# Moving vector-engine reductions, buffer clears and value-block steps to other places in the order of an attention and expert kernel

## Chip, cores and metric

The kernel runs on one core of a Trainium2 chip. The metric is the device time of one execution in microseconds (us).

## What is computed

Block-sparse attention for 2 batches, 8 heads, 768 positions and 64 channels, and behind it a layer of 8 experts with a top-1 router and a capacity. The reference, cut to what matters:

```python
k_sum = k.reshape(B, H, nb, block, D).max(axis=3)       # block = 32, nb = 24
v_sum = v.reshape(B, H, nb, block, D).mean(axis=3)
mask_l = np.abs(pos[:, None] - pos[None, :]) < window    # window = 16
scores_all = softmax over [masked local scores, scale * q @ k_sum.T + log(block)]
x = (a @ concat(v, v_sum)) as (1536, 512)

expert_idx = np.argmax(x @ w_gate, axis=1)               # gate_w: softmax at expert_idx
# each expert takes its first `capacity` (384) tokens in order
h = np.maximum(np.einsum('ecd,edf->ecf', disp, w1), 0.0)
y = np.einsum('ecf,efd->ecd', h, w2)
out[i] = gate_w[i] * y[expert_idx[i], pos[i]]            # 0 for tokens beyond the capacity
```

## The kernel before

**Chunks and groups.** The attention is worked off in 8 chunks c (a batch and a pair of heads). For each, SyncE loads keys `kc` (operation k), queries `qc` (q), values `v` (v) and the turned values `vc` (t). Each chunk has three groups n = 3c, 3c+1, 3c+2 of four query tiles. A group has five steps: S (L286, L287: scores and mask on TensorE), M (L291: negated row maximum on VectorE), E (L295: exponentials on ScalarE), R (L300: transposes on TensorE) and K (L304: copy to SBUF on ScalarE). V (L314) is the product with the values for one half of a chunk (V00 and V01 are the halves of chunk 0, V40 and V41 those of chunk 4), N (L322, L325) normalises it on VectorE into X.

**Inputs of a chunk.** w and kp (L229 on GpSimd) copy key windows and key-block maxima into the tile `k`; kb (L256) is the key-block maximum on VectorE. Q..v, Q..p and Q..a scale one head's queries into the tile `qb`, on VectorE, GpSimd or ScalarE. A `qb` is block-diagonal, and z2 and z3 (L222, L223) clear buffers 2 and 3 of it on GpSimd, two instructions each; buffers 0 and 1 are cleared ahead of the loop. vb (L263) sums the value blocks on VectorE, vt (L266) turns the sums on TensorE into `bank`, vk (L269) copies them to `vrow` on ScalarE, vP and vp (L229, out v<-vrow) copy them behind the values on GpSimd.

**Routes and rounds.** The first batch's 768 tokens are routed as soon as their attention is done: x, X, l, L, g (logits), ch (choice, VectorE), pf (counts and prefix sums on TensorE, into `bank`), pick (the two fullest experts of the first half, ending with the clip of the counts, `pcl`, L448), pl (places: the row maps `rowm` L425 and the column maps `colm` L428 on VectorE), tk0 (L457: product of both maps on TensorE, into `bank`), rows (`apk` L487, `aids` L494: row numbers of the expert's tokens), pads (L774 to L503), ts0 (L837) and fr0 to fr2 (L573: gathers by GpSimd's DMA queue). An expert round then works on these 384 rows while the second batch is routed: h and s split the weights, T, H, I turn and split the rows, u, r, e are the first layer (L627), D the second (L644), P scatters the result. There are three rounds. zr clears a tile of zeros that fill0 and fill1 write to the output.

**What sets the order.** Every engine works off its own queue in order. The order comes from one table, `SEQ`, whose names are called one after the other; a generator such as `pick`, `rows`, `pads`, `pl0` issues one instruction per call. Waits between engines are added by the framework from the tiles that an instruction reads and writes. `bank` is one PSUM tile with corners for logits, counts, prefix sums, the turned value sums and the token tables, and accesses of different engines to it are ordered as accesses to one tile:

```python
    bank = psum.tile([P, 4 * P], F32, name="bank", bufs=1)
    vtrn = corner(P)[:, 0]
    tbs = [corner(E, J), corner(E, J)]
```

Of the kernel before, what the change touches and what calls it, by code (L numbers as in the profile page):

```python
# [109 lines left out]


SEQ = """
q1 k1 t0 S0 k2 z2 t2 S1 M0 E0 Q11v q2 M1 Q10p w1p q3 kb1 E1 S2 kp1p vb0 R0 z3 R1 M2 t1 E2 K0 S3 K1 k3 kb2 v0 w2p vt0 M3 v2 vk0 vb2 S4 kp2p E3 v1 R2
Q21a M4 S5 q4 Q20p K2 t3 E4 Q30p vP0 k4 R3 M5 Q31a vp0 S6 vb1 E5 misc t4 R4 M6 w3p q6 S7 K3 kb3 v3 E6 vt1 M7 V00 kp3p q5 vk1 K4 V01 vp1 N00 N00 vP1 R5
N01 N01 E7 S8 K5 R6 M8 S9 K6 E8 R7 M9 vt2 vk2 V10 E9 vP2 V11 N10 N10 Q41a Q40p S10 N11 N11 K7 vp2 k5 vb3 R8 S11 M10 t5 K8 w4p kb4 E10 R9 M11 vt3 kp4p
V20 vk3 K9 vP3 V21 N20 E11 vb4 S12 vp3 N21 t6 N20 Q60p k6 Q61a N21 R10 M12 k7 R11 K10 S13 E12 vt4 K11 M13 V30 vk4 V31 E13 Q50p N30 N30 S14 N31 Q51a
N31 w5p kb5 R12 x0 M14 K12 kp5p x1 vb5 X0a x2 X1a S15 t7 vb6 X2a q7 E14 v6 vt5 M15 l00 w6p vk5 kb6 v5 R13 L00a E15 R14 w7p v4 kb7 x3 g00 K13 v7 S16
X3a kp6p vb7 K14 vP4 x4 M16 x5 Q70p X4a S17 X5a vp4 Q71a vt6 kp7p E16 M17 l01 vp5 R15 vP5 L01a E17 S18 vk6 g01 K15 M18 vp6 R16 ch0 S19 vP6 E18 ch0 ch0
ch0 ch0 R17 ch0 ch0 M19 S20 ch0 ga0 E19 ga0 ga0 pf0 ga0 pick pick pick M20 pick pick pick first lw0 lw1 lw2 lw3 vt7 V40 vk7 pl0 K16 pl0 vP7 V41 N40
pl0 K17 N40 S21 N41 vp7 zr N41 pl0 pl0 pl0 R18 pl0 pl0 E20 R19 V50 pl0 pl0 pl0 pl0 K18 M21 V51 K19 N50 N50 E21 pick tk0 S22 N51 N51 ts0 pads rows pads  # L120
R20 rows pads M22 rows fr0 S23 K20 pads E22 pads pads pads firstB R21 fr1 M23 K21 V60 E23 V61 fr2 N60 N60 h10a R22 N61 N61 R23 K22 s10v V70 K23 h11a
V71 lW0 lW1 lW2 lW3 fill0 N70 N70 x6 x7 X6a x8 X7a N71 N71 s11v x9 X8a h12p T0 x10 H0 X9a l10 X10a h13p x11 L10a T1 I0 X11a T2 H1 g10 H2 I1 l11 I2
L11a u0 s12v g11 s13v lwB0 lwB1 lwB2 lwB3 o0 o1 o2 h20a u1 ch1 ch1 r0 ch1 e0 ch1 ch1 ch1 ch1 ch1 pf1 ga1 ga1 ga1 ga1 u2 r1 e1 pl1 pl1 pl1 pl1 h21a u3
pl1 pl1 pl1 pl1 r2 e2 pl1 pl1 pl1 pl1 cl1 s20v h22a u4 r3 e3 tk1 ts1 rowsB rowsB frB0 frB1 frB2 u5 h23a r4 e4 s21v s22v u6 r5 e5 s23v padsB padsB
# [847 lines left out]
```

## Time and profile before

| | |
|---|---|
| median of 3 runs | 191.23 us (191.14 to 191.71) |
| the profiled execution | 192.58 us, span 190.5 us |
| TensorE matmul | 173.9 us busy, 91% of the span |
| VectorE | 105.3 us, 55% |
| ScalarE | 102.2 us, 54% |
| GpSimd | 61.7 us, 32% |
| DMA | 38.77 MB, mean 204 GB/s |

The span runs from the first to the last instruction; the profiled execution's own time is 2.08 us more. In the timeline a row is one instruction or several alike in a run, with the idle time of its engine ahead of it and what ended that. PE is TensorE, PEld its weight loads, DVE VectorE, ACT ScalarE, POOL GpSimd, SP SyncE.

### The profile page before, as it was taken

The numbers are of one execution on the slowest core, as the hardware profiler recorded it, in microseconds if no ns is written. First come the engines' busy times: TensorE is split into PE (matmuls) and PEld (weight loads), VectorE is DVE, ScalarE is ACT, GpSimd is POOL, SyncE is SP. The second block draws the span as 40 slices with busy tenths as digits, with TensorE's granted clock in tenths as the row PEclk, the third lists the DMA queues.
The fourth block names the chain that finished last, engine by engine and source line by source line (L and its number), as shares of the span: only waits on it lengthen the run. The fifth ranks groups of instructions, "written<-read, shape, count | busy, mean of one in ns | idle before, by whom it ended". The sixth has DMA issues, their size and how long they took to land. (4 is left out here: it accounts for less than half of the span.)

```text
span 190.5 us, 3991 instructions
## 1 busy us (share of the span) xinstructions
PE 173.9 (91%) x1461; PEld 155.7 (82%) x1461; DVE 105.3 (55%) x226; ACT 102.2 (54%) x225; POOL 61.7 (32%) x82
## 2 busy tenths in 40 slices
PE   6767999999999699899999999999999999999950
PEld 2556899999789697799998889999888899988830
DVE  3585658697279867579798658554610933210000
ACT  4549989999966496746343476444523722211110
POOL 7599528856634183000240522400022020002220
PEclk9999999999999999999999999999999999999995
DMA  5999999938949799999165899990010110001011
GB/s 169 333 322 269 256 336 288 347 139 272 276 124 322 222 341 402 401 386 368 59 163 162 315 387 383 375 369 4 0 55 0 57 59 0 0 2 57 25 40 57
DMA packets 20375, 38.77 MB, mean 204 GB/s; under 512 B 1482, under 2 KB 8572, under 8 KB 20348
## 3 DMA queue, kind: packets, MB, share of 16 engines
q1 hardware_dynamic: 18416, 33.43, 53.2%
q0 software_dynamic: 1440, 4.73, 6.8%
q10 hardware_dynamic: 492, 0.28, 0.6%
q8 instruction: 13, 0.21, 0.4%
q14 instruction: 14, 0.11, 0.2%
HBM read 29.77 MB, written 8.66 MB: 202 GB/s over the span
## 5 line engine op out<-in xcount | busy, mean ns | idle before, releaser
L644 PE MATMUL yp<-w,h 128*128 128x512 f32 x216 | 50.5, 391 | 0.0
L644 PEld LDWEIGHTS yp<-w,h 128*128 128x128 f32 x216 | 40.3, 188 | 8.2
L627 PE MATMUL hp<-xh,w1h 128*128 128x384 f32 x96 | 32.7, 340 | 0.0
L627 PE MATMUL hp<-xh,w1l 128*128 128x384 f32 x96 | 32.2, 335 | 0.0
L627 PE MATMUL hp<-xl,w1h 128*128 128x384 f32 x96 | 32.1, 335 | 0.0
L295 ACT ACTIVATE prob<-sc,nm 128x120 f32<-128x120 f32 x96 | 26.9, 369 | 8.5 <-DVE nm L291 4.6
L286 PE MATMUL sc<-k,qb 128*128 128x120 f32 x192 | 26.5, 281 | 4.4 <-ACT prob L295 1.4
L657 POOL DMA_INDIRECT out<-y,oid x9 | 9.8, 1094 | 60.5 <-ACT y L654 57.5
L286 PEld LDWEIGHTS sc<-k,qb 128*128 128x128 f32 x192 | 23.3, 191 | 6.7 <-ACT prob L295 2.0
L632 ACT ACTIVATE h<-hp 128x384 fp32r<-128x384 f32 x24 | 11.8, 492 | 29.6 <-PE hp L627 29.6
L636 DVE SCALAR_TENSOR_TENSOR h<-hp,h 128x384 fp32r<-128x384 f32 x24 | 13.3, 553 | 18.1 <-ACT h L632 18.1
L291 DVE TENSOR_REDUCE nm<-sc 128x4 f32<-128x480 f32 x24 | 15.7, 655 | 13.2 <-PE sc L287 7.6
L654 ACT ACTIVATE y<-yp,xgb 128x512 f32<-128x512 f32 x9 | 6.2, 687 | 28.4 <-PE yp L644 18.9
L627 PEld LDWEIGHTS hp<-xh,w1h 128*128 128x128 f32 x96 | 18.0, 188 | 0.3 <-issue 0.2
L627 PEld LDWEIGHTS hp<-xl,w1h 128*128 128x128 f32 x96 | 18.0, 188 | 0.1
L588 DVE TENSOR_TENSOR w<-w2r,w 128x1024 fp32r<-128x1024 f32 x12 | 14.6, 1227 | 6.1 <-ACT w L233 5.4
L627 PEld LDWEIGHTS hp<-xh,w1l 128*128 128x128 f32 x96 | 18.0, 188 | 0.0
L229 POOL TENSOR_SCALAR v<-vrow 25x1040 f32<-25x1040 f32 (+1 forms) x16 | 13.4, 840 | 10.0 <-ACT vrow L269 9.2
L582 DVE TENSOR_TENSOR w1l<-w1r,w1h 128x1024 fp32r<-128x1024 f32 x12 | 15.1, 1272 | 2.9 <-ACT w1h L233 2.7
L304 ACT COPY pts<-pt 121x512 f32<-121x512 f32 x24 | 13.9, 605 | 3.4 <-PE pt L300 2.6
L300 PE MATMUL pt<-cft,prob 128*121 128x128 f32 x96 | 14.3, 279 | 0.0
L233 ACT CAST w<-w2r 128x1024 fp32r<-128x1024 f32 x12 | 12.6, 1051 | 3.1 <-PE yp L644 2.4
(123 smaller groups left out, 223.1 us busy)
## 6 DMA issues: line engine op xcount, KB each, us to landing
w1r<-w SPq DMA_DIRECT2D x12, 512.0 KB, 7.0
w2r<-w SPq DMA_DIRECT2D x12, 512.0 KB, 6.0
v<-vw SPq DMA_DIRECT2D x16, 292.5 KB, 8.2
kc<-kT SPq DMA_DIRECT2D x8, 400.0 KB, 5.6
xrow<-x SPq DMA_DIRECT2D x2, 1542.0 KB
vc<-vT SPq DMA_DIRECT2D x8, 384.0 KB, 6.2
out<-zrow SPq DMA_DIRECT2D x2, 1536.0 KB, 12.9
qc<-qT SPq DMA_DIRECT2D x7, 384.0 KB, 6.4
```

The costliest lines, as they stand in the source:

```text
L229: eng.tensor_scalar(out=dst, in0=src, scalar1=f, scalar2=0.0, op0=ALU.mult, op1=ALU.add)
L233: nc.scalar.copy(out, in_)
L286: nc.tensor.matmul(self.sc[:, i, :], qb[c % NQ][:, t, :], kt[c][:, t, :], start=i == 0, stop=False)
L291: nc.vector.tensor_reduce(out=self.nm, in_=self.sc, op=ALU.max, axis=AX.X, negate=True)
L295: nc.scalar.activation(self.pr[:, i, :KW], self.sc[:, i], AF.Exp, bias=self.nm[:, i : i + 1])
L300: nc.tensor.transpose(self.pt[:KV, P * i : P * i + P], self.pr[:, i], ident)
L304: nc.scalar.copy(self.pts[:KV], self.pt[:KV])
L582: eng.tensor_tensor(out=self.w1l[g], in0=self.w1r[g], in1=self.w1h[g].bitcast(F32), op=ALU.subtract)
L588: eng.tensor_tensor(out=self.w2[g][:, 1], in0=self.w2r[g], in1=self.w2[g][:, 0].bitcast(F32), op=ALU.subtract)
L627: nc.tensor.matmul(ps, a[g][:, kk, fo : fo + P], x[:, kk, :], start=n == 0, stop=n == 3 * KD - 1)
L636: nc.vector.scalar_tensor_tensor(out=h[:, f % 2, 1], in0=self.hp[f], scalar=0.0, in1=h[:, f % 2, 0].bitcast(F32), op0=ALU.max, op1=ALU.sub ...
L644: nc.tensor.matmul(ps, self.h[g][:, i, a, P * j : P * j + P], self.w2[g][:, w, i, :], start=n == 0, stop=n == 3 * KF - 1)
```

## The change

Only the table `SEQ` changes; it has the same 641 names before and after. Five things move:

- z2, which stood behind the load k2, and z3, which stood behind R0, go behind E2.
- vb0 goes behind M2 (it stood ahead of R0), E2 ahead of K0, S3 ahead of K0, kb2 behind M3, S4 ahead of vb2.
- The seventh call of pick, the clip of the counts, goes from ahead of tk0 to ahead of the place steps pl0.
- vt7, vk7, vP7, vp7 and zr go from around V40 to behind R19.
- Two calls of rows go from between the calls of pads to right behind tk0.

Two places of the table:

```diff
-E1 S2 kp1p vb0 R0 z3 R1 M2 t1 E2 K0 S3 K1 k3 kb2 v0 w2p vt0 M3 v2 vk0 vb2 S4 ...
+E1 S2 kp1p R0 R1 M2 vb0 E2 z2 z3 t1 S3 K0 K1 k3 v0 w2p vt0 M3 kb2 v2 vk0 S4 vb2 ...
...
-first lw0 lw1 lw2 lw3 vt7 V40 vk7 pl0 K16 pl0 vP7 V41 N40 pl0 K17 N40 S21 N41 vp7 zr N41 ...
+pick first lw0 lw1 lw2 lw3 V40 pl0 K16 pl0 V41 N40 pl0 K17 N40 S21 N41 N41 ...
...
-R18 pl0 pl0 E20 R19 V50 ... E21 pick tk0 S22 N51 N51 ts0 pads rows pads R20 rows pads ...
+R18 pl0 pl0 E20 R19 vt7 vk7 vP7 vp7 zr V50 ... E21 tk0 rows rows S22 N51 N51 ts0 pads pads R20 pads ...
```

GpSimd at the front, before (`qb_95` are chunk 1's queries, `k_183` its keys, `qb_96` and `qb_97` are the buffers that z2 and z3 clear):

```order
L229 TENSOR_SCALAR qb_94<-qc_114 64x4x64 x3
L222 MEMSET qb_96 64x12x64
L223 MEMSET qb_96 64x12x64
L229 TENSOR_SCALAR qb_95<-qc_147 64x12x64
L229 TENSOR_SCALAR k_183<-kc_149 128x12x64
L229 TENSOR_SCALAR k_183<-kc_149 128x12x32
L229 TENSOR_SCALAR k_183<-ks 128x12x24
L222 MEMSET qb_97 64x12x64
L223 MEMSET qb_97 64x12x64
L229 TENSOR_SCALAR k_239<-kc_159 128x12x64
```

and with the change (`k_181` is chunk 1's keys here):

```order
L229 TENSOR_SCALAR qb_94<-qc_114 64x4x64 x3
L229 TENSOR_SCALAR qb_95<-qc_147 64x12x64
L229 TENSOR_SCALAR k_181<-kc_149 128x12x64
L229 TENSOR_SCALAR k_181<-kc_149 128x12x32
L229 TENSOR_SCALAR k_181<-ks 128x12x24
L222 MEMSET qb_96 64x12x64
L223 MEMSET qb_96 64x12x64
L222 MEMSET qb_97 64x12x64
L223 MEMSET qb_97 64x12x64
L229 TENSOR_SCALAR k_237<-kc_159 128x12x64
```

Chunk 1's four copies now stand ahead of all four clears, and chunk 2's keys follow the clears.

VectorE at the front, before (the rows are M1, kb1, vb0, M2, kb2, M3, vb2):

```order
L291 TENSOR_REDUCE nm<-sc 128x4
L256 TENSOR_REDUCE ks<-kc_149 128x24
L263 TENSOR_REDUCE vsq_85<-vc_151 128x24
L291 TENSOR_REDUCE nm<-sc 128x4
L256 TENSOR_REDUCE ks<-kc_159 128x24
L291 TENSOR_REDUCE nm<-sc 128x4
L263 TENSOR_REDUCE vsq_85<-vc_163 128x24
```

and with the change:

```order
L291 TENSOR_REDUCE nm<-sc 128x4
L256 TENSOR_REDUCE ks<-kc_149 128x24
L291 TENSOR_REDUCE nm<-sc 128x4
L263 TENSOR_REDUCE vsq_85<-vc_151 128x24
L291 TENSOR_REDUCE nm<-sc 128x4
L256 TENSOR_REDUCE ks<-kc_159 128x24
L263 TENSOR_REDUCE vsq_85<-vc_161 128x24
```

M2 and M3 each changed places with the reduction ahead of them.

TensorE around the first route's counts (the rows of `pf0` end above; `vsq_86` holds the sums that vt7 turns, `v_751` and `v_729` are the values of chunks 4 and 5), the piece of the difference:

```order
 L401 MATMUL bank<-oh,crt 128x8
-L266 MATMUL bank<-cft,vsq_86 128x128
 L314 MATMUL av<-v_751,pts 64x65 x24
 L286 MATMUL sc<-k_748,qb_97 128x120 x4
...
 L300 MATMUL pt<-cft,prob_83 121x128 x4
 L300 MATMUL pt<-cft,prob_84 121x128 x4
+L266 MATMUL bank<-cft,vsq_86 128x128
 L314 MATMUL av<-v_729,pts 64x65 x24
 L457 LDWEIGHTS rowm
```

vt7 goes from behind the counts to behind R19, and so vk7 on ScalarE goes from ahead of K16 to behind E20. On GpSimd nothing changes its place there: vP7, vp7 and zr stay the rows ahead of the gathers. SyncE's queue has the same rows in the same order.

VectorE from the column maps on, before:

```order
L428 TENSOR_TENSOR colm<-kt_967,eqj 128x6x24 x2
L291 TENSOR_REDUCE nm<-sc 128x4
L322 RECIPROCAL rz<-av 128x6
L325 TENSOR_TENSOR x_99<-av,rz 128x3x128
L448 TENSOR_SCALAR pcl<-bank 128x8
L322 RECIPROCAL rz<-av 128x6
L325 TENSOR_TENSOR x_99<-av,rz 128x3x128
L774 TENSOR_TENSOR mine_1089<-pcl,eq_919 128x8
L487 TENSOR_TENSOR apk<-bank,eq_919 128x24
L776 TENSOR_REDUCE c_1090<-mine_1089 128x1
L494 TENSOR_REDUCE aids<-apk 128x3
L501 TENSOR_TENSOR apad<-cft,c_1090 128x3
```

and with the change, to M22:

```order
L428 TENSOR_TENSOR colm<-kt_967,eqj 128x6x24 x2
L291 TENSOR_REDUCE nm<-sc 128x4
L322 RECIPROCAL rz<-av 128x6
L325 TENSOR_TENSOR x_99<-av,rz 128x3x128
L487 TENSOR_TENSOR apk<-bank,eq_919 128x24
L494 TENSOR_REDUCE aids<-apk 128x3
L322 RECIPROCAL rz<-av 128x6
L325 TENSOR_TENSOR x_99<-av,rz 128x3x128
L774 TENSOR_TENSOR mine_1093<-pcl,eq_919 128x8
L776 TENSOR_REDUCE c_1094<-mine_1093 128x1
L501 TENSOR_TENSOR apad<-cft,c_1094 128x3
L291 TENSOR_REDUCE nm<-sc 128x4
```

The clip `pcl` is gone from here (it stands ahead of the place steps now), and the row numbers `apk` and `aids` stand ahead of the last normalisation.

## Rows read from the trace of the kernel before

**Rows 1.** Windows: stretch, length, busy of PE, PEld, DVE, ACT, POOL, clock, DMA, GB/s.
```profile
...
24.00:56.00 32.00, 31.41 (x406) 29.13 (x403) 21.92 (x44) 27.80 (x78) 19.42 (x27) 1.00 0.87 264
...
73.00:180.00 107.00, 106.34 (x628) 96.89 (x628) 55.13 (x112) 45.61 (x70) 14.99 (x15) 1.00 0.48 172
...
```

**Rows 2.** PE timeline, front: start, length, engine, line, operation, out<-in, shapes, count, [idle<-releaser].
```profile
...
9.75 0.33 PE L287 MATMUL sc<-cmt 128*128 128x384 bf16 x1
...
12.27 1.15 PE L286 MATMUL sc<-k,qb 128*128 128x120 f32 x8 [1.04 <-POOL k L229]
...
22.55 1.62 PE L314 MATMUL av<-v,pts 121*64 121x65 f32 x48
...
```

**Rows 3.** Timeline of POOL (GpSimd), front.
```profile
...
7.82 0.73 POOL L222 MEMSET qb<- 64x768 f32 x1
8.59 1.05 POOL L223 MEMSET qb<- 64x768 f32 x1
9.73 0.82 POOL L229 TENSOR_SCALAR qb<-qc 64x768 f32<-64x768 f32 x1
10.52 1.30 POOL L229 TENSOR_SCALAR k<-kc 128x768 f32<-128x768 f32 x2
11.79 0.42 POOL L229 TENSOR_SCALAR k<-ks 128x288 f32<-128x288 f32 x1
...
```

**Rows 4.** Timeline of DVE (VectorE), front.
```profile
...
8.02 0.95 DVE L229 TENSOR_SCALAR qb<-qc 64x768 f32<-64x768 f32 x1 [0.47 <-DMA qc<-qT]
...
11.39 0.95 DVE L263 TENSOR_REDUCE vsq<-vc 128x24 f32<-128x768 f32 x1 [0.75 <-DMA vc<-vT]
12.26 0.65 DVE L291 TENSOR_REDUCE nm<-sc 128x4 f32<-128x480 f32 x1
...
```

**Rows 5.** Timeline of ACT (ScalarE), front.
```profile
...
13.03 1.11 ACT L295 ACTIVATE prob<-sc,nm 128x120 f32<-128x120 f32 x4 [2.23 <-DVE nm L291]
...
```

**Rows 6.** Timeline of SP's queue: the load of the second half of v0.
```profile
...
13.70 0.42 SPq L219 DMA_DIRECT2D v<-vw  x1
```

**Rows 7.** DMA view of that load: tile, queue, operation, count, KB, us to landing.
```profile
...
v<-vw SPq DMA_DIRECT2D x1, 292.5 KB, 8.1
```

**Rows 8.** Timeline of PE, second place.
```profile
...
56.92 0.33 PE L266 MATMUL bank<-cft,vsq 128*128 128x128 f32 x1 [0.26 <-DVE key L737]
...
64.20 0.45 PE L457 MATMUL bank<-colm,rowm 128*128 128x24 bf16 x12 [1.74 <-DVE pcl L448]
...
```

**Rows 9.** Timeline of DVE, second place.
```profile
...
57.76 1.00 DVE L747 TENSOR_TENSOR at<-eq,cft 128x16 f32<-128x16 f32 x1
...
59.00 0.45 DVE L753 TENSOR_SCALAR ei<-k 128x2 int32<-128x2 f32 x1
...
61.42 0.95 DVE L425 TENSOR_TENSOR rowm<-crt,lo 128x768 bf16<-128x768 bf16 x1
62.29 0.52 DVE L428 TENSOR_TENSOR colm<-kt,eqj 128x144 bf16<-128x144 bf16 x2
...
65.21 0.15 DVE L501 TENSOR_TENSOR apad<-cft,c 128x3 f32<-128x3 f32 x1
65.83 0.66 DVE L291 TENSOR_REDUCE nm<-sc 128x4 f32<-128x480 f32 x1 [0.47 <-PE sc L287]
...
```

**Rows 10.** Timeline of POOL, second place.
```profile
...
57.68 1.74 POOL L229 TENSOR_SCALAR v<-vrow 25x1040 f32<-25x1040 f32 x2 [3.29 <-ACT vrow L269]
...
```

**Rows 11.** Timeline of ACT, second place.
```profile
...
60.19 1.11 ACT L295 ACTIVATE prob<-sc,nm 128x120 f32<-128x120 f32 x4 [1.20 <-PE pt L300]
...
66.80 1.12 ACT L295 ACTIVATE prob<-sc,nm 128x120 f32<-128x120 f32 x4
...
73.32 1.56 ACT L233 COPY xt<-xp 128x512 f32<-128x512 f32 x3 [1.06 <-PE xp L348]
```

**Rows 12.** Timeline of all engines at the second route.
```profile
...
92.97 2.41 DVE L588 TENSOR_TENSOR w<-w2r,w 128x1024 fp32r<-128x1024 f32 x2
...
94.12 1.05 POOL L573 DMA_INDIRECT xgb<-xrow,bids  x1 [21.02 <-DMA xrow<-x]
...
```

More of the change, by code (lines that the diff above doesn't have):

```diff
@@ L112 @@
 SEQ = """
-q1 k1 t0 S0 k2 z2 t2 S1 M0 E0 Q11v q2 M1 Q10p w1p q3 kb1 E1 S2 kp1p vb0 R0 z3 R1 M2 t1 E2 K0 S3 K1 k3 kb2 v0 w2p vt0 M3 v2 vk0 vb2 S4 kp2p E3 v1 R2
+q1 k1 t0 S0 k2 t2 S1 M0 E0 Q11v q2 M1 Q10p w1p q3 kb1 E1 S2 kp1p R0 R1 M2 vb0 E2 z2 z3 t1 S3 K0 K1 k3 v0 w2p vt0 M3 kb2 v2 vk0 S4 vb2 kp2p E3 v1 R2
 Q21a M4 S5 q4 Q20p K2 t3 E4 Q30p vP0 k4 R3 M5 Q31a vp0 S6 vb1 E5 misc t4 R4 M6 w3p q6 S7 K3 kb3 v3 E6 vt1 M7 V00 kp3p q5 vk1 K4 V01 vp1 N00 N00 vP1 R5
@@ L118 @@
 X3a kp6p vb7 K14 vP4 x4 M16 x5 Q70p X4a S17 X5a vp4 Q71a vt6 kp7p E16 M17 l01 vp5 R15 vP5 L01a E17 S18 vk6 g01 K15 M18 vp6 R16 ch0 S19 vP6 E18 ch0 ch0
-ch0 ch0 R17 ch0 ch0 M19 S20 ch0 ga0 E19 ga0 ga0 pf0 ga0 pick pick pick M20 pick pick pick first lw0 lw1 lw2 lw3 vt7 V40 vk7 pl0 K16 pl0 vP7 V41 N40
-pl0 K17 N40 S21 N41 vp7 zr N41 pl0 pl0 pl0 R18 pl0 pl0 E20 R19 V50 pl0 pl0 pl0 pl0 K18 M21 V51 K19 N50 N50 E21 pick tk0 S22 N51 N51 ts0 pads rows pads
-R20 rows pads M22 rows fr0 S23 K20 pads E22 pads pads pads firstB R21 fr1 M23 K21 V60 E23 V61 fr2 N60 N60 h10a R22 N61 N61 R23 K22 s10v V70 K23 h11a
+ch0 ch0 R17 ch0 ch0 M19 S20 ch0 ga0 E19 ga0 ga0 pf0 ga0 pick pick pick M20 pick pick pick pick first lw0 lw1 lw2 lw3 V40 pl0 K16 pl0 V41 N40 pl0 K17
+N40 S21 N41 N41 pl0 pl0 pl0 R18 pl0 pl0 E20 R19 vt7 vk7 vP7 vp7 zr V50 pl0 pl0 pl0 pl0 K18 M21 V51 K19 N50 N50 E21 tk0 rows rows S22 N51 N51 ts0 pads
+pads R20 pads M22 rows fr0 S23 K20 pads E22 pads pads pads firstB R21 fr1 M23 K21 V60 E23 V61 fr2 N60 N60 h10a R22 N61 N61 R23 K22 s10v V70 K23 h11a
 V71 lW0 lW1 lW2 lW3 fill0 N70 N70 x6 x7 X6a x8 X7a N71 N71 s11v x9 X8a h12p T0 x10 H0 X9a l10 X10a h13p x11 L10a T1 I0 X11a T2 H1 g10 H2 I1 l11 I2
```

## Prediction

> **What bounds the kernel now.** I read the busy time of the engines by stage first. From 24 to 56 us TensorE is busy for 31.41 of 32.00 us and from 73 to 180 us for 106.34 of 107.00, at granted clock 1.00 [rows 1]. In both stretches TensorE sets the pace, so whatever brings it there earlier stays saved, as long as its inputs come. All of the change lies ahead of them or between them: at 7 to 24 us and at 56 to 73 us. So I read those two places engine by engine in the timeline, to see which wait ends last.
>
> At the front, TensorE waits 1.04 us at 12.27 for the keys of chunk 1 from GpSimd [rows 2]. GpSimd was late because the two clears of z2 (0.73 us each) lay ahead of its three copies for chunk 1 [rows 3]. The exponentials E2 on ScalarE wait 2.23 us for the maximum M2 on VectorE [rows 5], and VectorE was late because it took the value sums vb0 first and waited 0.75 us there for a load, though the scores S2 had been ready since 9.75 + 0.33 = 10.08 us [rows 2, 4].
>
> At the second place TensorE waits 1.74 us at 64.20 for the clip of the counts, L448 [rows 8]. The clip has nothing to do with the product that waits: both use the tile `bank`, and the row maps and column maps which the product reads were done at 62.29 + 0.52 = 62.81 us [rows 9].
>
> **Front part: z2, z3, M2, M3, S4 (forecast 1.45 us gained).**
> Step 1, chunk 1 on GpSimd. Chunk 1's queries land at 8.0 us: VectorE's half starts on them at 8.02 [rows 4]. Without z2 ahead, GpSimd's half starts there too instead of at 9.73. The two halves get in each other's way: VectorE's half took 0.95 us beside the clears, and the second clear took 1.05 us beside it, against 0.73 for the first [rows 3, 4]. I take VectorE first, for 0.55 us (between 0.42, which is what was left of it after the first clear ended, and 0.95), then 0.82 on GpSimd: 9.4 us. The copies of 1.30 us follow to 10.7. VectorE meanwhile does M1 (0.65, as M2) and the key maxima kb1 (0.95, as vb0) by 10.1, so the last copy, 0.42 us, ends at 11.1, and the scores S3 start at 11.2 instead of 12.27: 1.1 us. If GpSimd goes first, VectorE is 0.8 us later and S3 starts at about 11.65.
> Step 2, M2 ahead of vb0. M2 can start at 10.15 and ends at 10.8 us. E2 then starts at 10.9 instead of 13.03: 2.1 us. vb0 still starts at 11.39, when its load is there [rows 4], so the load train behind it in SyncE's queue (t1, k3, v0) starts as before.
> Step 3, what is late next. From E2 on, ScalarE's exponentials and copies run in one queue, and that chain moves by up to 2.1 us. But the second half of the values v0 was issued at 13.70 and took 8.1 us, so it lands at 21.8 [rows 6, 7]. The products V01 that need it are the second half of a 1.62 us group that began at 22.55 [rows 2], so they began at about 23.36. They can begin at 21.85: 1.5 us, and 1.45 after a little friction at later loads. Moving z2 and z3 together behind chunk 1 costs GpSimd 4 x 0.73 = 2.92 us from 11.1 to 14.2. Chunk 2's copies then start some 0.4 us later than before, which the queries for S6 bear: they would be ready at 16.8, and S6 waits for E4 until 17.0. Bounds: 0.5 us if later loads eat most of it, 2.1 if v0 lands earlier too, since the load q3, freed by GpSimd's first copy, goes out 1.2 us sooner.
>
> **Second part: the clip, vt7, vk7 and the copies (forecast 0.15 us lost).**
> Taken alone, the clip's move gives 1.74 us, less what the column maps leave. And vt7 leaves its place, where TensorE waited 0.26 us and worked 0.33 [rows 8], so V40 starts at 56.6, and the exponentials E20, which started at 60.19 after a transpose [rows 11], at 59.6 us. VectorE gains too. At 57.76 its product with two SBUF inputs took 1.00 us, and the cast at 59.00 took 0.45, while GpSimd's value copies ran from 57.68 for 1.74 us [rows 9, 10]; a small product of the same kind alone, at 65.21, took 0.15 [rows 9]. With the copies gone from there, everything up to the row maps moves some 0.95 us ahead (0.8 and 0.3, less 0.15 for the clip): the row maps, which began at 61.42, run from 60.47 to 61.42.
> But the copies come back at a worse place. vt7 now runs after R19, E20 ends at 60.7, vk7 takes 0.26 us, and GpSimd starts on vP7 0.08 us later: 61.1 us, in the middle of the row maps. These and the column maps have two SBUF inputs as well. GpSimd waits for the row maps to end (61.4) and makes its first, larger copy in about 1.06 us (that of before held the product of 57.76 until 58.76). One column map of 0.26 us gets through, then the second copy takes the other 0.65, then the second column map follows: done at 63.5 instead of 62.81. A row at the second route shows such a change of hands: GpSimd's gather at 94.12 started between two of VectorE's products (2.41 us for two, from 92.97) and needed 1.05 us [rows 12].
> The Trainium skill, "SBUF — State Buffer", section "Who interferes with whom", has a rule for this that speaks against the change: a VectorE instruction with two SBUF inputs and a GpSimd instruction that reads SBUF shut each other out, and whichever issues first keeps the shared pair for its whole length. By it GpSimd (61.1) issues ahead of the column map (61.34), which makes the full collision the case; a rule that favoured the running engine would make the sum 1.5 us better. No row before shows this very pair.
> With the maps done at 63.5, tk0 ends at about 64.0 instead of 64.65, and S22 and R20 come 0.6 us earlier. That doesn't last. E22 on ScalarE began at 66.80, behind K20 [rows 11], and then needs M22. M22 waited for S22 until 65.83; it now stands behind M21, two normalisations, the row numbers and the pads. These took VectorE from 62.81 to 65.21 + 0.15 = 65.36, so 2.55 us [rows 9]; from 63.5, without the clip but with more waits on a result just made, they end near 66.2, and M22 (0.66) near 66.85. E22 starts at 66.95: 0.15 us later than before. ScalarE had its next gap at 73.32 - 1.06 = 72.26 [rows 11], so TensorE, which waits for its results, inherits these 0.15 us. Bounds: lost 0.4 (pads queue up worse), gained 1.5 (no collision).
> Costed at nothing: zr, a clear of 0.53 us, whose reader is a load far behind; the row numbers' earlier place, as the gathers they start have their rows long before the transposes; kb2 and vb2, whose loads and readers have more than 1 us to spare.
>
> **Sum.** 1.45 - 0.15 = 1.3 us. The profiled execution took 192.58 us, 0.7% above the median of 191.23, and its span 190.5; I take the difference only: 191.23 - 1.3 = **189.9 us**. What a measurement of this kernel tells from no change is about 0.3%, 0.57 us.
>
> **The rivals.**
> *The copies miss the maps.* vP7 starts later than 61.6, or VectorE keeps its turn. The column maps are then done at 61.9, tk0 at 62.4, E22 starts near 65.25: 1.5 us gained here, 188.2 in all; if only one copy gets between, 189.4. For it: 61.1 is a sum of seven small steps. Against it: it misses the end of the row maps by 0.3 us. Chance 0.27.
> *The front gain is eaten by the load train.* If the loads up to 41 us pace the attention, and TensorE's full share in rows 1 only looks like work, 0.3 to 0.7 us remain: 190.7 to 191.1. Against it: TensorE is idle for 0.59 us in all of 24 to 56 us. Chance 0.13.
> *Slower: vb0 falls behind M2 and the load train with it.* SyncE's next load waits for vb0. Should S2, and so M2, be late, each us that vb0 starts after 11.39 moves t1, k3 and v0 by one, and V01 too. It decides from 1.5 us on, vb0 at 12.9 (M2 ending after 12.9, where it ended before): then the front gives nothing, and 0.7 us more give 192. For it: VectorE takes its queue in order. Against it: 0.55 us of slack. Chance 0.05.
> *The clip doesn't free tk0.* Its first product now waits for vk7 instead (61.0 us), which is earlier than the maps, so that the wait is really gone; this is inside the forecast.
>
> **How the numbers follow.** Forecast 0.52, its own range 189.5 to 190.4; copies miss 0.27; train 0.13; slower 0.05; anything else 0.03. The range from 188.2 to 190.9 leaves out the slower case, half of the train and the fastest tail. Faster by over 0.3% (below 190.66): the forecast, the first rival and a fifth of the second, 0.82. Same: 0.13. Slower (above 191.80): 0.05.
>
> **What would show it.** S3 starts near 11.2, E2 near 10.9 and V01 near 21.85 in the profile after; GpSimd's last two value copies fall at 61.1 less the front gain, inside the row maps, and a column map is recorded with about 1 us. L457 waits for VectorE's column map, not for the clip. The forecast is wrong if the column maps keep their 0.26 us each, if V01 starts no earlier than 23, or if the lead at 24 us is gone at 56.

## The result, and the profile after

| | before | after |
|---|---|---|
| median beside each other, 7 runs each | 191.58 us (191.14 to 193.06) | 190.09 us (189.11 to 190.44) |
| ratio, 95% interval | | 0.9894 (0.9864 to 0.9924) |
| the profiled execution | 192.58 us, span 190.5 | 190.09 us, span 188.0 |

The medians differ by 1.49 us; by the interval the time is 0.8 to 1.4% lower. First the windows of the profile after (stretch, length, busy of PE, PEld, DVE, ACT, POOL, clock, DMA, GB/s):

```profile
24.00:56.00 32.00, 31.38 (x441) 29.09 (x442) 22.71 (x48) 28.07 (x79) 18.60 (x26) 1.00 0.86 260
56.00:73.00 17.00, 15.28 (x242) 13.81 (x237) 14.40 (x40) 12.03 (x31) 7.74 (x8) 1.00 1.05 352
73.00:180.00 107.00, 106.34 (x618) 96.63 (x618) 53.33 (x109) 43.78 (x67) 16.37 (x14) 1.00 0.45 163
```

The two long stretches are as full as before [rows 1]: TensorE lacks 0.62 us of 32 and 0.66 us of 107. So a lead that it has at 24 us can be read again at 180, if nothing between takes it.

The front after, in the timeline (start, length, engine, line, operation, out<-in, shapes, count, [idle<-releaser]), one engine after the other:

```profile
10.93 1.15 PE L286 MATMUL sc<-k,qb 128*128 128x120 f32 x8
...
20.58 1.62 PE L314 MATMUL av<-v,pts 121*64 121x65 f32 x48
...
7.45 0.82 POOL L229 TENSOR_SCALAR qb<-qc 64x768 f32<-64x768 f32 x1 [0.20 <-DMA qc<-qT]
8.67 1.31 POOL L229 TENSOR_SCALAR k<-kc 128x768 f32<-128x768 f32 x2 [0.40 <-DMA kc<-kT]
10.44 0.43 POOL L229 TENSOR_SCALAR k<-ks 128x288 f32<-128x288 f32 x1 [0.46 <-DVE ks L256]
...
10.28 0.65 DVE L291 TENSOR_REDUCE nm<-sc 128x4 f32<-128x480 f32 x1
10.84 0.94 DVE L263 TENSOR_REDUCE vsq<-vc 128x24 f32<-128x768 f32 x1
...
11.04 1.12 ACT L295 ACTIVATE prob<-sc,nm 128x120 f32<-128x120 f32 x4 [0.52 <-PE pt L300]
```

S3 starts at 10.93 instead of 12.27 and doesn't wait for GpSimd any more [rows 2], E2 at 11.04 instead of 13.03 [rows 5], and the first value product V00 at 20.58 instead of 22.55. That is a lead of 1.97 us. vb0 didn't wait for its load this time (no bracket; 0.75 us before [rows 4]).

The second place after:

```profile
58.21 0.27 PE L266 MATMUL bank<-cft,vsq 128*128 128x128 f32 x1
60.53 0.19 PE L457 MATMUL bank<-colm,rowm 128*128 128x24 bf16 x1 [0.49 <-DVE colm L428]
61.20 0.42 PE L457 MATMUL bank<-colm,rowm 128*128 128x24 bf16 x11 [0.49 <-DVE colm L428]
...
56.29 0.16 DVE L448 TENSOR_SCALAR pcl<-bank 128x8 f32<-128x8 f32 x1
58.44 0.95 DVE L425 TENSOR_TENSOR rowm<-crt,lo 128x768 bf16<-128x768 bf16 x1
59.31 1.84 DVE L428 TENSOR_TENSOR colm<-kt,eqj 128x144 bf16<-128x144 bf16 x2
63.79 0.65 DVE L291 TENSOR_REDUCE nm<-sc 128x4 f32<-128x480 f32 x1
...
59.16 1.83 POOL L229 TENSOR_SCALAR v<-vrow 25x1040 f32<-25x1040 f32 x2 [6.45 <-ACT vrow L269]
...
64.54 1.12 ACT L295 ACTIVATE prob<-sc,nm 128x120 f32<-128x120 f32 x4 [0.65 <-DVE apad L503]
```

The wait of 1.74 us for the clip is gone [rows 8]. In its place stand two of 0.49 us for the column maps, which took 1.84 us instead of 0.52 [rows 9], because GpSimd's two value copies ran beside them. E22 starts 2.26 us earlier than before [rows 11]: the front's lead and 0.3 us.

### The profile page after: what moved, and what is told of

Read it like the earlier page. It is cut to its first block, busy times and chain, and to the rows that moved or that the text cites. A ratio compares the mean times of both kernels' runs of the same rounds, so it can differ in the third digit from the quotient of the medians.

```text
span 188.0 us, 3993 instructions
## 1 busy us (share of the span) xinstructions
PE 174.0 (93%) x1461; PEld 155.8 (83%) x1461; DVE 105.7 (56%) x226; ACT 102.4 (54%) x225; POOL 62.1 (33%) x82
## 5 line engine op out<-in xcount | busy, mean ns | idle before, releaser
L627 PE MATMUL hp<-xh,w1h 128*128 128x384 f32 x96 | 32.7, 340 | 0.0
L627 PE MATMUL hp<-xh,w1l 128*128 128x384 f32 x96 | 32.2, 335 | 0.0
L627 PE MATMUL hp<-xl,w1h 128*128 128x384 f32 x96 | 32.1, 334 | 0.0
L657 POOL DMA_INDIRECT out<-y,oid x9 | 10.4, 1151 | 60.0 <-ACT y L654 57.5
L286 PE MATMUL sc<-k,qb 128*128 128x120 f32 x192 | 26.8, 283 | 2.9 <-POOL qb L229 1.7
L286 PEld LDWEIGHTS sc<-k,qb 128*128 128x128 f32 x192 | 23.5, 193 | 5.2 <-POOL qb L229 2.8
L627 PEld LDWEIGHTS hp<-xh,w1h 128*128 128x128 f32 x96 | 18.0, 188 | 0.3 <-issue 0.2
L627 PEld LDWEIGHTS hp<-xl,w1h 128*128 128x128 f32 x96 | 18.0, 188 | 0.1
L627 PEld LDWEIGHTS hp<-xh,w1l 128*128 128x128 f32 x96 | 18.0, 188 | 0.0
```

The costliest lines, as they stand in the source:

```text
L286: nc.tensor.matmul(self.sc[:, i, :], qb[c % NQ][:, t, :], kt[c][:, t, :], start=i == 0, stop=False)
L627: nc.tensor.matmul(ps, a[g][:, kk, fo : fo + P], x[:, kk, :], start=n == 0, stop=n == 3 * KD - 1)
```

## The experiments

Each kernel is a variant of the table SEQ of the kernel before ("front" is the first line of the diff above, "second part" the rest) or of the changed kernel. Three chips were used; the kernels of one chip share its runs of before, so microseconds are compared within a chip, and ratios across chips with some caution (the second part alone, below, shows how much).

### The front alone

```diff
-... kp1p vb0 R0 z3 R1 M2 t1 E2 K0 S3 K1 k3 kb2 v0 w2p vt0 M3 v2 vk0 vb2 S4 ...
+... kp1p R0 R1 M2 vb0 E2 z2 z3 t1 S3 K0 K1 k3 v0 w2p vt0 M3 kb2 v2 vk0 S4 vb2 ...
```

> Only the front part of the change (z2, z3, vb0, M2, E2, S3, kb2, vb2, S4); the first route stays as before. Theory (front chain): S3 starts near 11, V00 near 20.6 to 21.1 instead of 22.55, and the lead of 1.5 to 2 us is still there at the counts pf0 (56.34 before) and at the end: 189.6 to 190.1 us against 191.6, ratio 0.990 to 0.992. Rival (the loads pace the attention): the lead at V00 shrinks to under 0.5 us by pf0, ratio above 0.997. Rival (the change's gain lies in the clip's wait): ratio 1.000.

191.91 us against 192.62, ratio 0.9956 (0.9932 to 0.9981): 0.7 us gained, between the theory's 1.5 to 2 and the rival's nothing. V00 came at 20.46 us, as early as after. Yet the profiled span was 190.1 us, hardly under that of before. Some of the lead went on the way to pf0: from V00 this took 34.53 us instead of 33.79, 0.43 of it in a wait of chunk 1's products for their values. More went at the second place: after the wait for the clip, the granted clock was at its lower level. The two waits, the window at that level, and the eight products of S23 (L286) in it:

```profile
27.17 0.92 PE L314 MATMUL av<-v,pts 121*64 121x65 f32 x24 [0.43 <-DMA v<-vw]
...
62.86 0.45 PE L457 MATMUL bank<-colm,rowm 128*128 128x24 bf16 x12 [1.75 <-DVE pcl L448]
...
64.05:67.46 3.41, 3.41 (x18) 3.31 (x17) 0.73 (x2) 1.60 (x5) 2.23 (x2) 0.50 0.88 274
...
65.36 1.90 PE L286 MATMUL sc<-k,qb 128*128 128x120 f32 x8
```

The same products in before, at granted clock 1.00 (2.4 GHz):

```profile
66.07 1.05 PE L286 MATMUL sc<-k,qb 128*128 128x120 f32 x8
```

At granted clock 0.50 (1.2 GHz) they took 1.90 us instead of 1.05. The first turn x6 (L348) started 17.25 us after the counts pf0, and 15.66 in before: 1.6 us lost.

### The second part alone, twice

```diff
-... pick pick pick first lw0 lw1 lw2 lw3 vt7 V40 vk7 pl0 K16 pl0 vP7 ... E20 R19 V50 ... E21 pick tk0 S22 ...
+... pick pick pick pick first lw0 lw1 lw2 lw3 V40 pl0 K16 pl0 ... E20 R19 vt7 vk7 vP7 vp7 zr V50 ... E21 tk0 rows rows S22 ...
```

> Only the second part (clip, vt7, vk7, vP7, vp7, zr, rows); the front stays as before. Theory (the copies hit the column maps): the two column maps take about 1.8 us together, L457 starts some 0.6 to 1 us earlier than 64.20 counted from pf0, E22 is 0.3 us earlier at most: 0 to 0.5 us gained, ratio 0.997 to 1.000. Rival (the wait of 1.74 us is simply saved): 1.2 to 1.7 us gained, ratio 0.991 to 0.994.

192.01 us against 192.62, ratio 0.9978 (0.9948 to 1.0008), as the theory said. The same kernel once more, on the chip of the last four runs:

> The front of before, the second part of the change as it is. Theory (the collision, 0.8 us, takes most of the gain of the second part): ratio 0.996 to 0.999, 0.8 to 1.2 us above e11_midlate, and above the changed kernel by the front's 1 to 1.5 us. Rival (the front is worth little): within 0.4 us of the changed kernel.

190.49 us against 192.38, ratio 0.9917 (0.9889 to 0.9945): over twice the gain that the theory allowed. The two intervals don't quite meet: the second part is worth 0.2% on one chip and 0.8% on another. Their profiles differ in one thing at this place. e2_mid's TensorE stood still at about 69 us (0.41 us, then 0.18) and reached x6 at pf0 + 15.84; e12_mid's didn't, and reached it at + 14.87. These gaps are taken up below.

### The clip's move alone

```diff
-... pick pick pick first lw0 ... E21 pick tk0 S22 ...
+... pick pick pick pick first lw0 ... E21 tk0 S22 ...
```

> Kernel before with one edit: the clip goes ahead of the place steps; vt7, vk7, vP7, vp7, zr and rows stay where they were, so GpSimd's copies still meet the picks at 57.7 and not the maps. Theory: column maps keep 0.30 us each and end at about 62.95, L457 starts there instead of 64.20, M22 no longer waits for S22 but for the pads (65.3), E22 starts near 66.05 instead of 66.80: 0.7 us gained, ratio 0.995 to 0.998, more than the whole second part alone. Rival (the maps' collision doesn't matter because ScalarE sets the pace from 66 us): the same as the second part alone, within 0.2 us.

193.02 us against 192.62, ratio 1.0025 (0.9989 to 1.0061): nothing gained, where 0.7 us was expected. TensorE in the timeline:

```profile
57.00 0.33 PE L266 MATMUL bank<-cft,vsq 128*128 128x128 f32 x1 [1.79 <-DVE pcl L448]
...
62.48 0.46 PE L457 MATMUL bank<-colm,rowm 128*128 128x24 bf16 x12
...
67.79 0.36 PE L314 MATMUL av<-v,pts 121*64 121x65 f32 x4 [0.36 <-issue]
68.55 0.32 PE L314 MATMUL av<-v,pts 121*64 121x65 f32 x2 [0.40 <-issue]
```

tk0 doesn't wait at all, but vt7 (L266), which also writes `bank`, now waits 1.79 us for the clip. The wait has only moved. So the clip's move doesn't pay by itself, and vt7's move takes the next writer of `bank` off that spot. (vt7's move without the clip's wasn't run.)

### The copies behind the column maps

```diff
-... E20 R19 vt7 vk7 vP7 vp7 zr V50 ... tk0 rows rows S22 N51 ...
+... E20 R19 V50 ... tk0 rows rows S22 vt7 vk7 vP7 vp7 zr N51 ...
```

With the change's front:

> The changed kernel with vt7, vk7, vP7, vp7 and zr moved once more, behind tk0, rows and S22, so that GpSimd's copies run beside instructions that read PSUM. Theory: column maps 0.30 us each, L457 starts about 1.3 us earlier than in the changed kernel, M22 and E22 too: 1.0 to 1.4 us faster than the changed kernel, 188.7 to 189.1 us, ratio to before 0.983 to 0.987. Rival (the maps' collision costs nothing, since ScalarE's queue sets the pace there): as the changed kernel, 0.989 to 0.990.

190.23 us against 192.62, ratio 0.9874 (0.9832 to 0.9917). VectorE's column maps and GpSimd's copies in its timeline:

```profile
58.86 0.52 DVE L428 TENSOR_TENSOR colm<-kt,eqj 128x144 bf16<-128x144 bf16 x2
...
61.56 1.77 POOL L229 TENSOR_SCALAR v<-vrow 25x1040 f32<-25x1040 f32 x2 [9.57 <-ACT vrow L269]
```

The maps are back at 0.52 us, and x6 starts at pf0 + 14.61 instead of + 15.34 after: the collision cost 0.73 us there, less than the expected 1.0 to 1.4. With the front of before:

> The kernel before with the second part of the change alone, but vt7, vk7, vP7, vp7 and zr moved on behind S22. Theory (the value copies' collision with the column maps takes about 0.8 us of what the clip's move gives): no column map over 0.35 us, S22 about 2.8 to 3.2 us nearer to pf0 than before, x6 at pf0 + 14.6 to 14.9 instead of + 15.65, time 0.8 to 1.1 us under before, ratio 0.994 to 0.996. Rival (second place is not worth more because E22, M22 or the loads of w1r and w2r bind next): x6 at pf0 + 15.4 or more, ratio 0.998 to 1.000.

190.56 us against 192.76, ratio 0.9876 (0.985 to 0.9903), x6 at pf0 + 14.56. x6 came as the theory said, but the time fell by 2.2 us, twice the expected 0.8 to 1.1. That the front should bring nothing on top of this was the reason for the square below.

### One half of the front at a time

Only the clears, behind E2:

```diff
-... k2 z2 t2 ... R0 z3 R1 M2 t1 E2 K0 ...
+... k2 t2 ... R0 R1 M2 t1 E2 z2 z3 K0 ...
```

> The kernel before with only z2 and z3 moved behind E2. Theory (the two front moves need each other): GpSimd reaches chunk 1's copies without the clears, so S3 could start near 11.0 instead of 12.27, but M2 still stands behind vb0 on VectorE, so E2 starts near 12.5 to 13.0 as before, the chain of ScalarE does not move, V00 starts at 22.2 to 22.6 and the time is 0 to 0.4 us under the kernel before, ratio 0.998 to 1.000. Rival (each move brings its own share, the clears' being chunk 1's 1.1 us): V00 near 21.5 and the time 1 us lower, ratio 0.995.

Only the value sums and key maxima, behind M2 and M3:

```diff
-... kp1p vb0 R0 z3 R1 M2 t1 E2 K0 S3 K1 k3 kb2 v0 w2p vt0 M3 v2 vk0 vb2 S4 ...
+... kp1p R0 z3 R1 M2 vb0 t1 E2 K0 S3 K1 k3 v0 w2p vt0 M3 kb2 v2 vk0 S4 vb2 ...
```

> The kernel before with only vb0 behind M2 and kb2 behind M3, vb2 behind S4; the clears stay. Theory (ScalarE's chain from E2 on carries the front): E2 near 10.9, V00 0.8 to 1.2 us earlier than before (S3 stays at 12.2 behind the clears and holds E3, so not the whole 2 us), ratio 0.994 to 0.996. Rival (chunk 1's keys bind): E2 near 10.9, but E3 and with it V00 as before, ratio 0.999 to 1.000.

192.33 us and 192.31 against 192.76, ratios 0.9981 (0.9957 to 1.0005) and 0.9978 (0.9952 to 1.0003). Each is too small to tell from nothing, and the timelines say why. ScalarE with the clears moved, then TensorE with the sums moved:

```profile
11.81 1.12 ACT L295 ACTIVATE prob<-sc,nm 128x120 f32<-128x120 f32 x4 [1.38 <-DVE nm L291]
```

```profile
12.80 1.15 PE L286 MATMUL sc<-k,qb 128*128 128x120 f32 x8 [1.04 <-POOL k L229]
...
22.10 1.62 PE L314 MATMUL av<-v,pts 121*64 121x65 f32 x48
```

With the clears alone, S3 starts early (10.84), but E2 still waits for M2 behind vb0. With the sums alone, E2 starts without that wait (11.86), but S3 still waits 1.04 us for GpSimd. V00 came 14.97 and 15.04 us after the mask product of S0, against 15.12 in the mean of the six profiles with the old front (14.39 to 16.04). With the clears alone V00 follows vb0 by 11.17 us, as with the old front (below), so the chain behind vb0 hasn't changed. V00 itself came at 21.35, near the rival's 21.5, but only because vb0 started at 10.18 instead of 11.39. About the sums the rival is nearer. The timed runs don't settle it: the two halves' 0.43 and 0.45 us, each within its noise, add up to what the whole front gives below. That a half brings nothing rests on these traces.

### A square on one chip

The changed kernel beside the others, on two chips, then its variant with late copies and that with the old front:

> The changed kernel once more, beside the three others on one chip, so that parts and whole have the same runs of before. Theory (the parts add up: front by clears and sums together 0.85 to 2 us, second place 0.3): ratio 0.988 to 0.991, V00 near 20.6, pf0 near 54.4, x6 at pf0 + 15.3, column maps 1.1 and 0.7 us. Rival (its 2 us were partly a luckier landing of t0 and its first profile): V00 near 21.2, ratio 0.992 to 0.995.

> The changed kernel, as the corner of a square on one chip (front of before or of the change, by value copies before or behind the column maps). Theory (front lead of 1 to 2 us is kept to the end): ratio 0.989 to 0.992; the front is worth 0.5% over e12_mid. Also looked at: whether TensorE shows idle time put down to issue in the products V60 (0.4 us each, as in e3, e5, e6 and e8_changed) and x6 then at pf0 + 16.0 instead of + 15.3.

> The changed kernel with the value copies moved behind S22, beside the changed kernel on one chip. Theory (the collision with the column maps costs about 0.8 us): 0.6 to 0.9 us under the changed kernel, ratio to before 0.985 to 0.988, x6 at pf0 + 14.6. Rival (something later holds the end): within 0.3 us of the changed kernel.

> The front of before, the second part with the copies behind S22. Theory (front and second part add): 0.8 to 1.5 us above e10_late, ratio 0.992 to 0.995. Rival (the front's lead is worth little by the end, as e4_late and e7_midlate, 0.9874 and 0.9876 on two chips, suggest): within 0.4 us of e10_late.

e8_changed: 190.93 us against 192.76, ratio 0.9914 (0.9888 to 0.994). The other three ran on one chip with e12_mid, before at 192.38:

| second part | front of before | front of the change |
|---|---|---|
| as in the change | e12_mid 190.49, 0.9917 (0.9889 to 0.9945) | e9_changed 189.84, 0.9875 (0.9829 to 0.992) |
| copies behind S22 | e11_midlate 190.48, 0.9917 (0.9884 to 0.9949) | e10_late 189.45, 0.9864 (0.9814 to 0.9914) |

The front is worth 0.65 and 1.03 us. Late copies are worth 0.01 and 0.39 us, less than the expected 0.6 to 0.9, and their kernel can't be told from the changed one by these intervals. In e9_changed only the first copy hit the maps (1.16 and 0.30 us), and x6 lay at pf0 + 14.91, so 0.35 us was left to gain there. Nearly all of that is given back behind x6. In GpSimd's queue the gathers follow the copies; with late copies they started 10.4 us behind pf0 (e7, e10, e11) instead of 8.8 and 8.9 (e12, e9), and TensorE waited for the first gathered rows. In e10_late:

```profile
72.14 0.63 PE L601 MATMUL xgp<-cft,xgb 128*128 128x128 f32 x4 [0.46 <-DMA xgb<-xrow,aids]
```

e7 and e11 waited 0.58 and 0.55 us there, e9 and e12 not at all. By the first product of the first layer (L627) the late copies are no further than e9 and e12 (table below). The second part was worth 1.89 us here with the old front, and the whole change 2.54 us, against 1.83 on the chip of e8_changed.

## Why the prediction was right, and where its terms were off

The time came out as forecast: 190.09 us for 189.9, inside the range, and 1.49 us gained for 1.3. But the two terms didn't: the front was put too high and the second part too low, and the errors cancelled. That the sum fits is luck; on the two other chips the same kernel gained 1.83 and 2.54 us.

**What the profiles share.** Fourteen profiles, of before, after and the twelve runs, show how rigid the rest is. From V00 to pf0 it took 33.78 to 33.81 us in eleven of them (34.01 to 34.53 in the others), and from the first product of the first layer (L627) to the end 110.4 to 110.7 us in all. What is won stands at two places: ahead of V00, and between pf0 and L627. x6 lies in between, 7.4 to 8.2 us ahead of L627. (Gaps are idle times of TensorE in or just behind V60 that stay unexplained; see "Left open".)

| profiles | S0's mask product to V00 | pf0 to x6 | pf0 to L627 |
|---|---|---|---|
| old front: before, e2, e3, e7, e11, e12 | 14.39 to 16.04, mean 15.12 | | |
| new front: after, e1, e4, e8, e9, e10 | 13.89 to 14.08, mean 13.93 | | |
| clip behind the maps, no gaps: before | | 15.66 | 23.56 |
| the same, with gaps (e5, e6) or low clock (e1) | | 16.98 to 17.25 | 24.60 to 24.67 |
| clip moved alone, with gaps: e3 | | 17.07 | 24.79 |
| second part, no gaps, both copies among the maps: after | | 15.34 | 23.14 |
| second part, no gaps, one copy: e9, e12 | | 14.91, 14.87 | 22.58, 22.50 |
| second part, with gaps, one copy: e2, e8 | | 15.84, 16.02 | 23.57, 23.76 |
| copies behind S22: e4, e7, e10, e11 | | 14.56 to 14.61 | 22.52 to 22.77 |

**Front, steps 1 and 2: right, with sizes.** S3 was forecast at 11.2 and came at 10.93; E2 at 10.9 and came at 11.04. In after GpSimd took its half of chunk 1's queries first, not VectorE. Its copies were done early all the same, at 10.87, because it could start at 7.45 instead of the assumed 8.0; in the other five profiles with the new front VectorE's half took 0.56 us, as summed. By the traces of e5 and e6 neither half alone moves V00 out of the old front's range. The slack left for chunk 2's queries (0.2 us ahead of E4) was used up: they were done at 17.22, E4 at 17.17, and S6 started at 17.27.

**Front, step 3: this step failed.** It held V01 at 21.85 us because v0 was to land at 21.8, and that rested on "vb0 still starts at 11.39, when its load is there". In after vb0 started at 10.84, so v0 was issued at 13.13 instead of 13.70 and took 7.6 us instead of 8.1: it landed at 20.7, ahead of V01 (21.33). The load bounded nothing there. In the other direction the profile of before wasn't typical. With the old front V00 follows vb0 by 11.15 to 11.18 us in all six profiles, and vb0 started anywhere from 9.96 to 11.39; before's was the latest. So the front's 1.97 us between the two profiles is 15.12 - 13.93 = 1.19 us in the mean of six against six, and in the time 0.71 us in e1 and 0.65 to 1.03 in the square. The 1.45 of the forecast came from a wait of which one trace showed one draw.

**The collision: right in after, one draw of five.** Counted from the front's lead of 1.95 us, GpSimd's copies fell at 59.16 + 1.95 = 61.11 (forecast 61.1), and the row maps at 60.39 (forecast 60.47). The maps were done at 63.10 instead of 63.5. The two column maps took 1.84 us, held up by a copy each. By the rule that the prediction drew from the Trainium skill, "SBUF — State Buffer", section "Who interferes with whom", the second of such a pair is shut out for the whole length of the first; the trace agrees: the column maps are recorded with 1.16 and 0.76 us beside the copies, and take 0.52 for both without them in e4_late. But the full collision came in one of the five profiles with this second part. In the other four (e2, e8, e9, e12) the rival's half case came, to which the prediction gave 0.5 us less: the second map got ahead of the second copy and took 0.30 us, the copy 0.80 instead of 0.62. By x6 this was worth 0.4 to 0.5 us (14.87 and 14.91 against 15.34). The starts of the rows don't tell which comes: the second copy's lies 14 to 20 ns ahead of the second map's in all five.

**The second part's balance: this term had the wrong sign.** The forecast was 0.15 us lost at E22. In the profiled pair 0.3 us were gained there: the maps were done 0.4 us earlier than summed, and M22, behind them in VectorE's queue, started at 63.79 + 1.95 = 65.74 instead of 66.2. The larger part isn't in the profile of before at all. What stands between pf0 and x6 there, 15.66 us, is the best of the four profiles that have the clip behind the maps; the other three lost 1.3 to 1.6 us more, e1 to the clock and e5 and e6 to gaps in V60. The five profiles with the second part differ among themselves too, e2 and e8 by such gaps. By L627 the four stand at 24.36 us in the mean and the five at 23.11: 1.25 us gained, between the 0.61 and 1.89 us that were measured on two chips. Single profiles lie from 0.2 us lost (e8 against before) to 2.2 gained (e12 against e1). Why the two chips differ is not shown, since a timed run leaves no trace.

**The clock.** The forecast priced the wait for the clip at its 1.74 us alone. Each timed run lists its mean granted clock. It was 0.985 or less in 52 of 123 runs of the kernels in which TensorE waits over 1.7 us for the clip (before 30 of 75; e1, e3, e5, e6 22 of 48), and in 2 of 74 of those in which it doesn't. So a lower clock often goes with the wait, and with the change both are gone. The lists don't say where in a run the clock was low; only e1's profile shows that, behind the wait. What it costs isn't settled either. On the last chip (the square's) the runs of before with such a clock have a median of 192.71, the others 191.67; on the second (e5 to e8) it is 193.57 and 192.63, in e3 194.46 and 192.51. But on the first chip there was no such difference (192.53 and 192.71), nor in e1 (191.88 and 191.92), e5 and e6.

**That the clip frees tk0: right, but on a condition not given.** In e3_clip tk0 is free as well, and the wait stands ahead of vt7 instead. The prediction counted vt7's move as 0.26 us of wait and didn't see that the 1.74 us hang on it.

**The slower rival** didn't occur: vb0 started ahead of 11.39 in after, and later than that in one of six profiles with the new front (e10, 11.59), where S0's mask product itself came 0.9 us later than in after.

**Left open.** What the gaps in V60 are. They stand between the 755th and the 769th matmul of the program in all five profiles that have them (e2, e3, e5, e6, e8), the end of V60 and the transposes behind it: two or three of up to 0.47 us, put down to "issue" or to a releaser, with slow products between. By x6 they took 0.8 to 1.4 us (15.84 and 16.02 against the mean of 15.04 without, 16.98 and 17.02 against 15.66). e8_changed shows them in the very kernel whose other profiles don't have them:

```profile
65.89 0.34 PE L314 MATMUL av<-v,pts 121*64 121x65 f32 x4 [0.47 <-issue]
66.65 0.26 PE L314 MATMUL av<-v,pts 121*64 121x65 f32 x1 [0.42 <-issue]
```

The DMA engines are full at that time (398 GB/s from 64 to 68 us in e8), and one 16 KB packet of the queue that the page calls instruction runs within a microsecond of them, which suggests that TensorE waits for its instructions. But such a packet runs there in the profiles without gaps too, and no run took the load away, so this is argued and not shown. The seven profiles of the second part or of late copies that don't have these gaps have one of 0.43 us at the 785th matmul, in V70, put down to ScalarE's copy (in e4 to "issue").

## What to carry to other kernels

When a wait comes from a shared tile and not from data, look for the next writer of that tile: moving the reader alone moves the wait (1.74 us at tk0 became 1.79 us at vt7). Two reorderings that end at one meeting point, here GpSimd's copies and VectorE's maxima ahead of S3 and E2, can each leave the other's wait standing (in the traces V00 moved by 1.2 us only with both), so test them together before dropping either. And a stage whose start hangs on a load's landing should be read from several profiles: one trace gave a front of 16.04 us where six gave 14.39 to 16.04.

## What was not expected of the hardware

A wait of TensorE of 1.75 us was followed, 1.2 us after its end, by 3.41 us at granted clock 0.50, in a profile that otherwise holds 1.00 from 6 to 186 us; it happened in one profile of five with such a wait. Reordering also brought steadiness: V00 follows S0's mask product by 13.89 to 14.08 us with the new front, against a spread of 1.65 us with the old (six profiles each). And where GpSimd's copies met the column maps, with the first copy 4.77 to 4.78 us behind pf0 in all five profiles, one let GpSimd's second copy go first and four VectorE's second map.
